# A new written-out order and a new split between VectorE and GpSimd in a polysketch attention and feed-forward kernel

## The chip, the cores and the metric

The kernel runs on one core of a Trainium2 chip. The metric is the device time of one execution in microseconds (us), the median of several runs; lower is better.

## The reference

An attention block with a polynomial sketch feeds a multiplicative feed-forward block. There are 4 batches, 4 heads, 1088 positions per batch, a head dimension of 32 and a sketch of r = 8.

```python
def phi(x):                                   # S1, S2: 8 x 32
    a = np.einsum('rd,bhsd->bhsr', S1, x)
    b = np.einsum('rd,bhsd->bhsr', S2, x)
    return np.einsum('bhsi,bhsj->bhsij', a, b).reshape(*x.shape[:-1], r * r)
q_p, k_p = phi(q), phi(k)
kv = np.einsum('bhsf,bhsd->bhfd', k_p, v)
z = np.sum(k_p, axis=2)
num = np.einsum('bhsf,bhfd->bhsd', q_p, kv)
den = np.einsum('bhsf,bhf->bhs', q_p, z)[..., None] + 1e-06
attn = num / den
...
x = attn.transpose(0, 2, 1, 3).reshape(4352, 128)
a = x @ w1                                    # 128 x 1024
b = x @ w2
out = (a * b @ w3) @ w_out                    # 1024 x 1024, 1024 x 128
```

## The kernel before

The program is a set of named steps, and each step issues a few instructions. A long table, `ORDER`, names all 1181 steps one after the other; the driver issues them so and chains the instructions of each engine in that order, so no engine ever takes a later step first. Tables beside it say on which engine a step runs and in which buffer its result lies:

```python
    def on(name):
        return pool if name in POOL else act if name in ACTS else dve

    def cp(name):
        return dve.tensor_copy if name in CPV else act.copy
...
    for name in ORDER.split():
        n = len(traced)
        steps.pop(name)()
...
            if ins.engine in last:
                tc.add_manual_dep(ins, last[ins.engine].name, behind, reason="order")
```

`dve` is VectorE, `act` ScalarE, `pool` GpSimd, `pe` TensorE. `POOL` lists the steps that GpSimd does; what is in neither `POOL` nor `ACTS` is VectorE's. `CPV` lists the copies out of PSUM that VectorE does, the others are ScalarE's. `SLOTS` holds one string for each kind of buffer: the n-th tile of that kind lies in the buffer that the n-th character names, so a tile waits until the tile that had that buffer before has been read for the last time. Kind "b" are the eight PSUM banks; "raw" are the three buffers into which weights are loaded. `WARM` gives the number of idle bf16 products (128x256) in each of the steps `warm0`, `warm1` and so on, which keep TensorE at work.

How the work is tiled:

- **k side of a batch** (`k1.` is the second batch's): load, a largest value and a leading part on a coarse grid (`k1.lead0`, L214) and the rest (`k1.rest0`, L651), Gram products (`k1.gram0` to `gram4`, L659), a chain of very small steps (G, T, N: L201, L204, L865, L898 to L937), the result `Nr` (L954), transposed keys (L720), sketches `ab` (L727) with their transposes `abt` (L745), outer products `kp` (L677), and the sums over positions `kv` (L769).
- **q side of a chunk** (`q1.` is the second half of the first batch; `q2.` and `q3.` the second batch's halves; `q4.` and `q6.` the third and fourth batch, 1024 positions wide; `qr.` what is left of all): transposed queries `tr` (L1333); `rm` (L1352); sketch products A and C with their transposes `At` (L1385) and `Ct` (L1130, L1391); then on 128-row tiles `sm`, `st`, `sh` (L1137 or L1401, L201, L204), `sl` (L1157, L1417), `sc` or `scy` and `sca` (L1165, L1161, L1421), `al` (L1170, L1426), the parts of the denominator `p01` (L1176, L1432), `p2` (L1180, L1436), `p12` (L1184, L1440), their sum `dn` (L1189, L1445), `de` and `rc` (its reciprocal), `bs` (L1204, L1459), and the outer product `phi` (L1208, L1509). For q4 and q6 a norm stands between (`na` to `nn`: L217, L1474 to L1490). `phi` is transposed by VectorE (`pT`, L1517) or TensorE (`pt`, L1246), and multiplied by kv (`x`, L1297, L1527).
- **weights**: steps `w0` to `w10`: they come as 64-bit words in pieces (`load`, on SyncE's queue, L430 to L440), and are turned into f32 by ScalarE (`c`, `m`: L263, L462, L484), VectorE (`j`: L466, L495) and GpSimd (`a`: L470, L501). Steps `w0` and `w1` make one half each of the reference's w1 and w2 together, `w2` makes w_out, `w3` to `w10` the rows of w3. `f0` to `f7` multiply w3 by w_out first (`f6.t`, L528, transposes on VectorE; `f6.m`, L534, on TensorE), so that 1024 x 128 weights are left.
- **feed-forward**: groups of 512 tokens, `g0` to `g3`, each in eight pieces of the inner dimension: `g0.4a` (L1799, x by w1), `g0.4b` (L1809, x by w2), `g0.4c` (L1804, a copy of the first out of PSUM), `g0.4m` (L1815, VectorE, their product), `g0.4o` (L1835, the second layer, summed in PSUM). `g4` to `g7` belong to the second two batches and go through a scheme with seven products in place of eight (`h4.` and `h6.`, L1673 to L1785: products, `T` and `m` sums on VectorE or GpSimd, `P` products). `gr` is the rest (L1824).

In time the kernel does the first batch's keys and queries, then g0 and g1 with the second batch, then g2, g3 and the w3 products with the third and fourth batch's keys and queries, then h4, h6 and the rest.

Of the kernel before, what the change touches and what calls it, by code (L numbers as in the profile page):

```python
# [53 lines left out]
    g4.oS g5.oS g6.oS g7.oS h4.0T2 h4.0T3 h4.0T4 h4.0m11 h4.0m12 h4.0m22 h4.1T1 h4.1T3 h4.1m11  # L54
    h4.1m12 h4.2m11 h4.2m12 h4.2m22 h4.3T4 h4.s2 h6.0T1 h6.0T2 h6.0T4 h6.0m12 h6.0m22 h6.1T1 h6.1T2
    h6.1m11 h6.1m12 h6.1m22 h6.2T4 h6.2m11 h6.2m12 h6.s1 h6.s2 h6.s4 k0.Nf k0.Nh k0.Nr k0.kp1 k1.Nr
    k1.kp1 k2.Nr k2.kp0 k2.kp1 k2.rest0 k3.Nr k3.kp0 k3.kp1 q0.al q0.p01 q0.phi1 q0.sca q1.al q1.p01
    q1.p12 q1.phi q1.sca q2.bs q2.phi0 q3.al q3.bs q3.p01 q3.p12 q3.p2 q3.phi0 q3.sc q3.sl q4.nn
# [31 lines left out]
w0.m0 g0.0a g0.3a g0.2c k1.Ta k1.Tb s.RC k2.kT1 w0.a0 q1.pt0 k1.N0 q2.tr k1.Tc k1.N1 g0.6c q2.max k1.Na g0.0c w6.load  # L90
w2.load g0.6b g0.1a q1.pt1 k2.lead0 k2.rest0 q1.pc0 q1.pc1 q2.l2 q2.l1 q3.l1 g0.1b q1.x g0.5m q1.xT g0.3c g0.1c g0.1m
w9.m k1.Nr k2.gram0 k2.gram1 k2.gram2 k2.gram3 k2.gram4 k1.Nb k2.kT0 q3.rm q2.A0 q2.rm k1.kp0 k2.ab k2.abt q2.C0 q2.C1
g1.1a g1.1c v1.loadr k2.Gm q2.At q2.sm k2.Gt q2.Ct g1.5a w9.c k3.zero q2.st q3.A0 k2.Ga q3.C0 q3.C1 q3.Ct q2.sh k2.Gb
k3.load g1.7a v.s g1.7b g1.2a v1.load g1.7c q2.sl q2.sc q2.p01 q2.al q2.p2 k2.Gc q3.At g0.0b k1.kp1 q3.sm q3.st k1.kv0
q3.sh k2.T0 k1.kv2 k1.kv3 k1.kv1 k2.T1 k1.kvr k1.kvc kr1.kp g1.2c k2.Ta q2.p12 q2.dn q2.de k2.Tb g0.0m q2.rc g0.6m
q3.sl q3.sc q3.p01 w9.j g1.7m q1.restT q2.bs g1.6a g1.6c w2.c v2.zero q2.phi0 g1.2b k3.loadr g1.3a g1.3c g1.0a g1.5b
g1.3b k1.kqt warm12 w6.c w6.m g0.3b k1.kq g1.5c g1.4a k3.max g1.4c w5.load g1.1b v2.loadr kh3.load k0.Nr q2.load g1.3m
g1.5m g1.2m g1.0c q2.pT0 warm13 g1.0b k2.Tc q2.x g0.3m w9.a1 w5.m q2.xT0 k3.kT0 k2.N0 k2.N1 w5.c q3.al q3.p2 q3.p12
q3.dn w6.j g1.0m q3.de w7.load w2.m g1.4b w7.m w7.c w3.load w10.load w4.load v2.load w2.j k2.Na g1.4m k2.Nb q3.rc
k3.kT1 k3.lead0 q2.restT q3.bs g0.2b g2.6a g2.3a g2.1a g2.5a g2.4a g2.2a w5.j g1.1m g0.2m q3.phi0 k2.Nr g2.2b g2.0a  # L100
g2.3c g2.2c g2.4b g2.5c w3.c g1.6b k3.rest0 w9.a0 g2.4c w2.a0 g2.1c w2.a1 q4.tr k3.gram0 w6.a0 w5.a1 f6.t g2.2m
k3.gram1 k3.gram2 k3.gram3 k3.gram4 q3.pT0 f6.m g2.6b g2.6c g2.0c k3.Gm v.t g2.1b k3.Gt k3.Ga k3.Gb w7.j g2.4m q4.max
g2.7a g2.3b g1.6m q4.l2 w3.m k3.Gc w7.a0 g2.0b f6.o g2.3m w5.a0 w6.a1 v3.zero g2.1m q3.x q4.l1 k3.T0 k3.T1 g2.6m w3.j
g2.7c q4.rm g2.5b g2.5m q3.xT0 q3.load g2.7b g3.0a v3.load w8.load v3.loadr k3.Ta w4.m g3.0c g3.0b g3.0m g3.3a g3.1b
g3.1a g3.3c k3.Tb w3.a0 g3.1c g2.0m k2.kp1 q6.tr k3.Tc g2.7m w7.a1 f4.t g3.6a q3.restT g3.6c q4.A0 w3.a1 q6.max k3.ab
k3.N0 k3.abt k2.kp0 q4.C0 q4.C1 k3.N1 f4.m k3.kp1 g3.6b f0.t f3.t f4.o k3.kp0 f0.m q4.At q6.l2 g3.6m k2.kv0 k2.kv3
g3.1m w4.c w4.j k3.kv0 k3.kv1 k3.kv3 k3.kv2 k3.kvr q4.Ct q4.sm q6.l1 qr.max k3.kvc k2.kv1 k2.kv2 k2.kvr k2.kvc f3.m
w8.c f0.o f3.o w4.a1 w4.a0 g3.7a g3.7c g3.4b g2.0o k3.Na q4.st f1.t qr.l2 q6.rm q4.sh w10.m qr.l1 q4.sl q4.sc g3.5a
g3.4a g3.3b f1.m f1.o w10.c g3.4c g3.4m qr.rm k3.Nb q4.p01 w8.m q4.al k3.Nr k3.kqt g2.4o q6.A0 q6.C0 f2.t g3.3m q4.p2
v.3 q6.C1 k3.kq q6.At w8.j w8.a1 q6.Ct g2.6o g3.0o g3.4o qr.A0 qr.C0 qr.C1 qr.Ct q6.sm w10.j q6.st q6.sh q4.p12 w8.a0  # L110
g3.5b q6.sl w10.a1 q6.sc q4.dn qr.At g3.5c q4.de f5.t q4.rc g1.0o g1.1o q4.na q4.bs q4.nb f2.m q4.nm q4.nr qr.sm q6.al
q6.p01 q6.p2 g0.0o g0.1o q6.p12 f2.o g0.2o g0.6o k2.kqt g0.3o q4.ne g3.5m q4.nn q6.dn k2.kq f5.m f5.o g3.7b g3.2b
g1.6o g0.5o g0.4o w10.a0 qr.st f7.t f7.m g3.2a q4.phi0 q4.phi1 qr.sh qr.sl qr.sc f7.o q4.pT0 g3.2c q4.pT1 g2.5o g0.7o
g0.oT g3.2m g3.3o g2.3o q4.x q4.xT2 q6.de qr.p01 q6.rc q4.xT0 q6.bs q6.nb q6.na g2.2o g2.7o qr.al q6.nm q6.nr q6.ne
q6.nn v.1 q4.xT1 q6.phi0 q6.phi1 g1.4o o.S3 q4.xT3 g1.2o q6.pT0 g3.5o g3.7m q6.pT1 g1.3o q6.x qr.p2 q6.xT2 qr.p12
qr.dn qr.de g3.1o g1.7o g3.6o g2.1o qr.rc qr.bs q6.xT3 g1.5o q6.xT0 h4.s1 h4.s3 q6.xT1 q6.ns g3.7o g3.2o qr.phi0
qr.pT0 g1.oT qr.x h4.0b5 h4.0a1 qr.xT0 h4.1a1 g2.oT g2.st h4.0b2 g3.oT h4.0a5 h4.0b1 h4.0bd h4.1b1 h4.0ac h4.s2 h4.s4
h4.1ac v.2 h4.0a6 h4.0bc h4.0bh h4.0ae o.S1 h6.s1 h4.0a2 h4.0ah h4.0b3 h4.1b2 o.S2 o.S4 h4.0ad h4.1a6 h6.s2 h4.0a7
h4.0m11 h4.0b6 h4.1a5 g3.st h4.1bc h4.1b6 h4.1ae h4.1bh v.4 h4.0ag h4.0be h4.0bf h4.1b5 h4.0a3 h4.0af h4.0b7 h4.1a7
h4.1be h4.1b7 h4.1ad h4.0a4 h4.0m12 h4.1a2 h4.0bg h4.1bd h4.1b3 h4.1a3 h4.0m22 h4.0b4 h4.1ag h4.2b1 h4.0ai h4.2a1  # L120
h4.1bf h4.2bc h4.2b2 h4.1ah h4.1a4 h4.2a2 h4.2ac h4.1bg h4.1af h4.1m12 h4.1m22 h4.1b4 h4.3b1 h4.2a6 h4.1ai h4.0m21
g1.st h4.2b5 h4.2ae h4.3a1 h4.2bh h4.1m11 h4.2ah h4.1m21 h4.3bc h4.1T1 h4.2m11 h4.3ac h4.2b6 h4.2be h4.2bd h4.0T1
h4.2a5 h4.2ad h4.3a2 h4.3b2 h4.3bh h4.3b6 h4.2a7 h4.2b7 h4.0T3 h4.3a6 h4.3ae h4.2ag h4.2b3 h4.3ah h4.3be h4.2a3 h4.3a5
h4.3ad h4.3b5 h4.3bd h4.2bg h4.2a4 h4.3b7 h4.3a7 h4.1T3 h4.2af h6.1b1 h4.2bf h4.3m11 h4.3a3 h4.2m22 h4.3bg h4.2b4
h4.2ai h4.3ag h4.2m12 h4.3b3 h6.0a1 h4.2m21 h6.0ac h4.3af h4.3a4 h4.1T2 h6.1bc h4.3b4 h6.1a1 h6.0b1 h6.0a6 h4.3ai
h4.3m21 h6.1b6 h4.3bf h4.2T1 h6.1ac h4.0P7 h4.2P1 h4.1P7 h4.0T2 h4.0P1 h4.0T4 h4.1P2 h4.3T1 h4.3m22 h4.1P5 h4.0P4
h6.0bc h4.2P2 h4.0P2 h4.3P5 h4.3m12 h4.2P5 h4.1P6 h4.2T2 h4.2P6 h4.0P5 h4.2T3 h4.1P1 h4.3T3 h4.3P7 h4.2P7 h4.3P1
h4.3T2 h4.3T4 h4.3P6 h4.2T4 h4.2P4 h6.0ae h4.0P6 h4.3P4 h4.1T4 h6.s3 h4.1P4 h4.k1 h4.k3 h4.3P2 h4.k2 h4.0P3 h4.3P3
h4.2P3 h4.k4 h4.k7 h4.1P3 h6.1be h4.k5 gr.1a h6.0b6 gr.1c h6.0be h6.0a7 h6.0b5 h6.0a5 h6.1a6 h6.0ad h6.1b7 h4.k8 h6.s4
# [1805 lines left out]
```

## Time and profile before

| what | value |
|---|---|
| time, median of 3 runs | 250.13 us (249.65 to 250.77) |
| the profiled execution | 248.89 us, span 246.9 us |
| TensorE (PE) busy | 238.4 us (97%) |
| VectorE (DVE) busy | 212.2 us (86%) |
| ScalarE (ACT) busy | 121.8 us (49%) |
| GpSimd (POOL) busy | 154.4 us (63%) |
| TensorE clock | 1.000 of full |
| from HBM, to HBM | 19.40 MB, 2.23 MB |

The span is from the first to the last instruction; the execution's time holds some 2 us more around it. A timeline row gives start, length, engine, line, operation, what is written and read, their shapes and the number of instructions in a run of like ones; in square brackets stands how long the engine had been idle before, and which instruction ended that. An f32 product of 128 columns by 512 appears as two records.

### The profile page before, as it was taken

The numbers are of one execution on the slowest core, as the hardware profiler recorded it, in microseconds if no ns is written. First come the engines' busy times: TensorE is split into PE (matmuls) and PEld (weight loads), VectorE is DVE, ScalarE is ACT, GpSimd is POOL, SyncE is SP. The second block draws the span as 40 slices with busy tenths as digits, with TensorE's granted clock in tenths as the row PEclk, the third lists the DMA queues.
The fourth block names the chain that finished last, engine by engine and source line by source line (L and its number), as shares of the span: only waits on it lengthen the run. The fifth ranks groups of instructions, "written<-read, shape, count | busy, mean of one in ns | idle before, by whom it ended". The sixth has DMA issues, their size and how long they took to land.

```text
span 246.9 us, 6753 instructions
## 1 busy us (share of the span) xinstructions
PE 238.4 (97%) x2726; PEld 133.7 (54%) x2726; DVE 212.2 (86%) x426; ACT 121.8 (49%) x246; POOL 154.4 (63%) x198
## 2 busy tenths in 40 slices
...
GB/s 202 267 167 324 173 204 185 92 229 135 244 177 230 183 230 142 3 4 0 3 0 0 3 1 3 54 73 4 0 0 0 3 11 74 1 0 3 0 53 96
DMA packets 31934, 22.06 MB, mean 89 GB/s; under 512 B 21280, under 2 KB 26528, under 8 KB 31904
## 3 DMA queue, kind: packets, MB, share of 16 engines
...
q8 instruction: 21, 0.34, 0.6%
...
HBM read 19.40 MB, written 2.23 MB: 88 GB/s over the span
## 4 chain that ended last, share of the span: by engine, by line
PE 80%; DVE 15%; issue 2%; POOL 1%; ACT 0%; DVEq 0%
PE ps_X L1673 11%; PE ps_o L1759 10%; PE a_ps L1799 9%; PE b_ps L1809 9%; PE ps_o L1835 9%; PE ps_w3o L534 6%; PE ps_Y L1673 6%; PE idle_ps L255 4%; PE ps_Z L1673 3%; DVE ab L1815 3%; PE ps_g L659 2%; PE ps_ac L1374 2%; PE ps_kv L769 2%; PE ps_or L1824 2%; DVE pT L1517 1%
## 5 line engine op out<-in xcount | busy, mean ns | idle before, releaser
L1809 PE MATMUL b_ps<-xT,w 128*128 128x512 f32 (+1 forms) x80 | 36.4, 560 | 0.3 <-DVE ab L1815 0.2
L1673 PE MATMUL ps_X<-xd,wv 64*128 64x512 f32 x112 | 35.6, 595 | 0.0
L1799 PE MATMUL a_ps<-xT,w 128*128 128x512 f32 (+1 forms) x80 | 35.4, 558 | 0.0
L1804 ACT COPY ffa<-a_ps 128x512 f32<-128x512 f32 (+1 forms) x34 | 17.6, 536 | 30.4 <-PE a_ps L1799 30.3
L1680 ACT COPY hc<-ps_X 128x512 f32<-128x512 f32 x37 | 20.7, 589 | 21.2 <-PE ps_X L1673 12.9
L1835 PE MATMUL ps_o<-ab,w3o 128*128 128x512 f32 x64 | 29.4, 597 | 0.0
L1815 DVE TENSOR_TENSOR ab<-ffa,b_ps 128x512 f32<-128x512 f32 (+1 forms) x40 | 23.9, 619 | 3.2 <-PE b_ps L1809 2.5
L501 POOL TENSOR_TENSOR w3c<-w3c,cv_m 128x512 int32<-128x512 int32 x16 | 21.0, 1328 | 6.3 <-DVE w3c L495 6.3
L1799 PEld LDWEIGHTS a_ps<-xT,w 128*128 128x128 f32 x80 | 14.4, 190 | 14.6 <-issue 8.5
L1707 POOL TENSOR_TENSOR hc<-hc 128x512 f32<-128x512 f32 x15 | 19.7, 1327 | 2.9 <-DVE hc L1685 2.9
L1673 PEld LDWEIGHTS ps_X<-xd,wv 64*128 64x128 f32 x112 | 15.2, 186 | 10.4 <-issue 8.3
L1809 PEld LDWEIGHTS b_ps<-xT,w 128*128 128x128 f32 x80 | 14.0, 190 | 12.2 <-issue 7.7
L1673 PE MATMUL ps_Y<-xd,wv 64*128 64x512 f32 x48 | 19.2, 599 | 0.0
L1835 PEld LDWEIGHTS ps_o<-ab,w3o 128*128 128x128 f32 x64 | 11.7, 190 | 13.7 <-issue 13.2
L534 PEld LDWEIGHTS ps_w3o<-wo,w3T 128*128 128x128 f32 x128 | 15.3, 192 | 3.2 <-issue 2.5
L534 PE MATMUL ps_w3o<-wo,w3T 128*128 128x128 f32 x128 | 15.9, 277 | 0.6 <-DVE w3T L528 0.6
L1540 ACT COPY xd<-ps_x 64x256 f32<-64x256 f32 x32 | 11.7, 367 | 7.6 <-PE ps_x L1527 7.2
L538 ACT COPY w3o<-ps_w3o 128x128 f32<-128x128 f32 x8 | 2.0, 270 | 26.3 <-PE ps_w3o L534 26.3
L1759 PE MATMUL ps_o<-hc,w3o 128*64 128x512 f32 x32 | 14.7, 596 | 0.0
L1848 POOL TENSOR_TENSOR oT<-oT,nz 128x512 f32<-128x512 f32 x4 | 4.2, 1049 | 15.6 <-DVE oT L1842 14.4
L263 ACT ACTIVATE cv_c<-raw 128x1024 f32<-128x1024 f32 (+1 forms) x13 | 13.0, 1010 | 1.5 <-DMA raw<-in_moe_w_dram 1.5
L1509 POOL TENSOR_TENSOR ph<-s_al,s_bs 128x1024 f32<-128x1024 f32 x5 | 10.4, 2096 | 4.6 <-issue 4.5
...
## 6 DMA issues: line engine op xcount, KB each, us to landing
...
```

The lines of the kernel that those rows point to most:

```text
L263: act.activation(dst, hi.bitcast(F32), ACT.Prelu, scale=2.0 ** -112, alpha=-2.0 ** 32)
L501: pool.tensor_tensor(d, d, x["m"][:, i * 512:(i + 1) * 512], ALU.add)
L534: pe.matmul(t["o"], w3T[ko][:, c], wo[:, c], start=c == 0, stop=c == NC - 1)
L1673: pe.matmul(x[bank], stat(j, u)[:, i * 128:(i + 1) * 128], rows(j, u), start=new, stop=True, tile_position=(u * 64, 0), skip_group_check=True)
L1680: cp(n(y))(x[k], x[bank])
L1707: on(f"h{g}.{i}m{k}").tensor_mul(both[0][k], both[0][k], both[1][k])
L1759: pe.matmul(acc_o[bank][half[0]:half[1]], w(i), x(i), start=n == 1, stop=n == (2 if j == 3 else 4), tile_position=(0, half[0]), skip_group ...
L1799: pe.matmul(x["a"][:, :w], w_of(0, c), xT[g][:, c0:c0 + w], start=True, stop=True)
L1804: cp(f"g{g}.{c}{su}c")(x["s"][:, :w], x["a"][:, :w])
L1809: pe.matmul(x["b"][:, :w], w_of(1, c), xT[g][:, c0:c0 + w], start=True, stop=True)
L1815: dve.tensor_mul(ab_sb[g, c][:, c0:c0 + w], x["s"][:, :w], x["b"][:, :w])
L1835: pe.matmul(o_ps[g], w3o[:, c], ab_sb[g, c], start=n == 1, stop=n == NC)
```

## The change

Only tables change. `ORDER` is the same up to the step `q0.xT1`, that is until the first chunk of queries, q0, is through; behind it all steps stand in a new order. The first instructions that differ run at about 26.7 us. `POOL`, `CPV` and `SLOTS` go with the new order: 29 steps move from VectorE to GpSimd, 18 from GpSimd to VectorE, 12 copies from ScalarE to VectorE and 10 from VectorE to ScalarE. The planner that wrote the tables counted with long holds between VectorE and GpSimd. The last two entries of `WARM`, one idle product each, are gone with their steps.

```diff
-WARM = [27, 2, 3, 4, 4, 4, 1, 2, 1, 1, 2, 2, 1, 1]
+WARM = [27, 2, 3, 4, 4, 4, 1, 2, 1, 1, 2, 2]
...
-    "raw": "012012021020121",
+    "raw": "012011012121202",
...
 POOL = set("""
...
-    q4.p2 q4.phi0 q4.phi1 q4.sc q6.al q6.p12 q6.phi1 q6.sc q6.sl qr.p01 qr.p12 s.KS s.Pp s.blk
+    q3.p12 q3.p2 q3.phi0 q3.sc q4.al q4.p01 q4.p12 q4.p2 q4.phi0 q4.phi1 q4.sl q6.bs q6.p12 q6.p2
...
-w0.load k1.lead0 q0.xc0 q0.xc1 k0.kq w1.a1 k2.max q0.xt1 k1.ab q0.xT0 q0.xT1 g0.4a q1.load g0.5a q1.sm q1.Ct q1.st
-q1.sh k1.rest0 w0.m1 g0.4b g0.6a q1.sl q1.scy q1.sca g0.7a q1.p01 q1.al k1.abt k1.gram0 k1.gram1 k1.gram2 k1.gram3
+w0.load k1.lead0 q0.xc0 q0.xc1 k0.kq w1.a1 k2.max q0.xt1 k1.ab q0.xT0 q0.xT1 g0.4a q1.load s.RC g0.5a q1.sm q1.st
+k1.abt g0.4b k1.rest0 q1.sh g0.7a q1.Ct w0.c1 g0.4c w0.c0 kr1.abc w0.m1 k1.gram0 g0.7c k1.gram1 q3.tr k1.gram2 w0.j1
...
```

Three places show what moves. The first is VectorE from 26.3 us on, at the second half of the first batch's queries (s_g, s_t, s_hl, s_pr), the second batch's keys (kk, kabt) and a weight (w_81, j). Before:

```order
L1137 TENSOR_REDUCE s_g<-ps_a 128x32
L1130 STREAM_TRANSPOSE ay_C<-ps_c 128x384
L201 SCALAR_TENSOR_TENSOR s_t_699<-s_g,ps_a 128x256
L204 SCALAR_TENSOR_TENSOR s_hl<-s_g,s_t_699 128x2x128
L651 TENSOR_TENSOR kk<-k,kk 128x1152
L1157 TENSOR_TENSOR s_hl<-ps_a,s_hl 128x2x128
L1165 TENSOR_TENSOR s_hl<-s_hl,ay_C 128x128
L745 STREAM_TRANSPOSE kabt<-ps_ab 128x256 x2
L1180 TENSOR_TENSOR s_pr<-s_al,s_hl 128x128
L466 TENSOR_SCALAR w_81<-cv_c 128x2x256
L1333 STREAM_TRANSPOSE qT<-qh 128x512
L217 TENSOR_REDUCE G_g<-ps_g 128x1
```

In the changed kernel:

```order
L1137 TENSOR_REDUCE s_g<-ps_a 128x32
L201 SCALAR_TENSOR_TENSOR s_t_700<-s_g,ps_a 128x256
L745 STREAM_TRANSPOSE kabt<-ps_ab 128x256 x2
L651 TENSOR_TENSOR kk<-k,kk 128x1152
L204 SCALAR_TENSOR_TENSOR s_hl<-s_g,s_t_700 128x2x128
L1130 STREAM_TRANSPOSE ay_C<-ps_c 128x384
L1333 STREAM_TRANSPOSE qT<-qh 128x512
L466 TENSOR_SCALAR w_81<-cv_c 128x2x256
L1157 TENSOR_TENSOR s_hl<-ps_a,s_hl 128x2x128
L1165 TENSOR_TENSOR s_hl<-s_hl,ay_C 128x128
L1176 TENSOR_TENSOR s_pr<-s_hl 128x256
L466 TENSOR_SCALAR w_81<-cv_c 128x2x256
```

The transposes kabt and ay_C, kk and qT and the weight step change places with q1's chain: s_hl (L1157) was the sixth step and is now the ninth, and the product s_pr (L1176) is new here.

The second place is GpSimd at the same time, where q1's chain (s_hl, s_pr, s_al, ph) meets weights (w_81, a) and the second and third batches' kk (L651). Before:

```order
L470 TENSOR_TENSOR w_81<-w_81,cv_m 128x2x256 x2
L1161 TENSOR_TENSOR s_hl<-s_hl,ay_C 128x128
L1176 TENSOR_TENSOR s_pr<-s_hl 128x256
L1170 TENSOR_TENSOR s_al<-s_hl 128x128
L1184 TENSOR_TENSOR s_pr<-s_pr 128x128
L470 TENSOR_TENSOR w_81<-w_81,cv_m 128x2x256
L577 MEMSET v 64x4x32
L1208 TENSOR_TENSOR ph<-s_al,s_bs 128x1024
L378 COPY RC<-Sc 128x4x8 x3
L470 TENSOR_TENSOR w_81<-w_81,cv_m 128x2x256
L651 TENSOR_TENSOR kk<-k,kk 128x1152
```

In the changed kernel:

```order
L470 TENSOR_TENSOR w_81<-w_81,cv_m 128x2x256 x2
L378 COPY RC<-Sc 128x4x8 x3
L1161 TENSOR_TENSOR s_hl<-s_hl,ay_C 128x128
L1170 TENSOR_TENSOR s_al<-s_hl 128x128
L1180 TENSOR_TENSOR s_pr<-s_al,s_hl 128x128
L1184 TENSOR_TENSOR s_pr<-s_pr 128x128
L470 TENSOR_TENSOR w_81<-w_81,cv_m 128x2x256
L1204 TENSOR_TENSOR s_bs<-ay_C,s_rc 128x128
L1208 TENSOR_TENSOR ph<-s_al,s_bs 128x1024
L954 TENSOR_TENSOR AR<-RC,mask2n 128x2x8
L577 MEMSET v 64x4x32
L470 TENSOR_TENSOR w_81<-w_81,cv_m 128x2x256
```

The copies RC come first, s_pr (L1176) has gone, and s_pr (L1180) and s_bs (L1204) have come from VectorE, the latter just ahead of ph.

The third place is VectorE at the fourth batch's queries, q6: the norm (s_d, nz), the outer product ph and its transposes pT. Before, behind the transposes of q4:

```order
L1459 TENSOR_TENSOR s_bs<-ay_C,s_rc 128x256
L217 TENSOR_REDUCE s_d<-s_bs 128x32
L217 TENSOR_REDUCE s_d<-s_al 128x32
L1426 TENSOR_TENSOR s_al<-s_hl 128x64
L1474 TENSOR_TENSOR s_d<-s_d 128x32
L1480 TENSOR_REDUCE nz<-s_d 128x8
L1484 TENSOR_SCALAR nz<-nz 128x8
L1485 TENSOR_SCALAR nz<-nz 128x8
L1490 TENSOR_TENSOR s_bs<-s_bs,nz 128x256
L1509 TENSOR_TENSOR ph<-s_al,s_bs 128x1024
L1517 STREAM_TRANSPOSE pT<-ph 128x1024
L1815 TENSOR_TENSOR ab<-ffa,b_ps 128x512
```

In the changed kernel, from the second transpose of q4 on:

```order
L1517 STREAM_TRANSPOSE pT<-ph 128x1024
L217 TENSOR_REDUCE s_d<-s_bs 128x32
L1474 TENSOR_TENSOR s_d<-s_d 128x32
L1480 TENSOR_REDUCE nz<-s_d 128x8
L1484 TENSOR_SCALAR nz<-nz 128x8
L1485 TENSOR_SCALAR nz<-nz 128x8
L1490 TENSOR_TENSOR s_bs<-s_bs,nz 128x256
L1509 TENSOR_TENSOR ph<-s_al,s_bs 128x1024
L1517 STREAM_TRANSPOSE pT<-ph 128x1024
L1445 TENSOR_REDUCE s_d<-s_pr 128x2x8
L1517 STREAM_TRANSPOSE pT<-ph 128x1024
```

The steps s_bs (L1459) and s_al (L1426) are gone from VectorE here, a sum (L217) lies further ahead, and g3.7m (L1815) stood between the two last transposes and now stands behind them.

More of the change, by code (lines that the diff above doesn't have):

```diff
@@ L53 @@
 POOL = set("""
[L54 to L58, printed above, removed]
-    q4.p2 q4.phi0 q4.phi1 q4.sc q6.al q6.p12 q6.phi1 q6.sc q6.sl qr.p01 qr.p12 s.KS s.Pp s.blk
-    s.blkh s.low s.rest
+    g4.oS g6.oS g7.oS h4.0T1 h4.0T2 h4.0T3 h4.0m11 h4.0m12 h4.0m22 h4.1T3 h4.1m11 h4.1m12 h4.1m22
+    h4.2T3 h4.2m12 h4.2m22 h4.s2 h4.s3 h4.s4 h6.0T1 h6.0T2 h6.0T3 h6.0m12 h6.0m22 h6.1T1 h6.1T3
+    h6.1m11 h6.1m12 h6.1m22 h6.2T3 h6.2T4 h6.2m11 h6.2m22 h6.s2 h6.s3 h6.s4 k0.Nf k0.Nh k0.Nr k0.kp1
+    k1.Nr k1.kp0 k1.kp1 k2.kp0 k2.kp1 k2.rest0 k3.Nr k3.kp0 k3.kp1 q0.al q0.p01 q0.phi1 q0.sca q1.al
+    q1.bs q1.p12 q1.p2 q1.phi q1.sca q1.sl q2.al q2.p01 q2.p2 q2.phi0 q2.sc q2.sl q3.al q3.bs q3.p01
+    q3.p12 q3.p2 q3.phi0 q3.sc q4.al q4.p01 q4.p12 q4.p2 q4.phi0 q4.phi1 q4.sl q6.bs q6.p12 q6.p2
+    q6.phi1 qr.al qr.bs qr.p01 qr.p12 qr.p2 qr.phi0 qr.sc s.KS s.Pp s.blk s.blkh s.low s.rest
 """.split())
@@ L90 @@
[L90 to L129, printed above, removed]
@@ new lines @@
+q1.sl k1.gram3 q1.scy k1.gram4 k1.Gc q1.sca q1.p01 g0.6b kh2.load w0.j0 g0.4m g0.6a q3.max q1.al q1.p2 q1.p12 q1.dn
+k1.Gm g0.5c w0.a1 g0.2a g0.0a k1.Gt q1.de q1.rc s.AR w0.m0 k1.Ga k1.Gb k1.T0 q1.bs q1.phi k1.T1 k2.lead0 g0.3a g0.0c
+k0.Nr g0.5b w2.load q3.l2 v2.zero g0.7b k2.kT1 w9.load g0.2c q1.pt0 w6.load k1.Ta k1.Tb g0.6c g0.3c k1.Tc k1.N0 w2.m
+k1.N1 w0.a0 g0.1a k2.kT0 q1.restT k1.Na q2.tr g0.1c k2.rest0 q1.pt1 g0.1b q1.pc0 q1.pc1 q1.x k2.gram0 k2.gram1 q2.max
+k1.kp1 k1.Nb q2.l2 g0.1m g0.5m k3.zero k3.load g0.7m k1.Nr k2.gram2 k2.gram3 q3.l1 q2.l1 q3.rm k2.gram4 q1.xT w6.c
```

91 lines of the change are left out of this document (63 added, 28 removed).

## The prediction

> **What bounds the kernel now.** I read the page first: busy times, then the chain that ended last.
>
> ```profile
> PE 238.4 (97%) x2726; PEld 133.7 (54%) x2726; DVE 212.2 (86%) x426; ACT 121.8 (49%) x246; POOL 154.4 (63%) x198
> PE 80%; DVE 15%; issue 2%; POOL 1%; ACT 0%; DVEq 0%
> ```
>
> TensorE is at work for 238.4 of 246.9 us, at full granted clock, and 80% of the chain is its own. The change leaves every product in place except two idle ones. So the time can only move by TensorE's waits, and by how often VectorE (86%) or GpSimd (63%) comes late. The windows say in which stages that is:
>
> ```profile
> 140.00:151.00 11.00, 9.52 (x143) 4.12 (x142) 9.74 (x22) 5.87 (x17) 4.74 (x8) 1.00 0.01 2
> 151.00:247.00 96.00, 92.20 (x478) 46.14 (x478) 80.59 (x132) 36.94 (x79) 60.56 (x72) 1.00 0.14 24
> 240.74 2.50 PE L1824 MATMUL ps_or<-w3o,ab 128*128 128x128 f32 x20
> ```
>
> Columns of the first two: window, length, then busy time of PE, PEld, DVE, ACT, POOL. The third row is TensorE's last one in its timeline. Between 140 and 151 us TensorE stands for 1.5 us. From 151 us on it lacks 3.8, and 3.7 of that lie behind its last product, which ends at 243.24 of 246.9: in the stage itself it practically never waits. The timeline of TensorE gives the single waits, and a row without one gives the rhythm:
>
> ```profile
> 69.60 4.03 PE L1799 MATMUL a_ps<-xT,w 128*128 128x512 f32 x9
> 38.62 0.24 PE L912 MATMUL ps_N<-T_p,P2a 32*32 32x8 f32 x8 [0.22 <-DVE T_p L204]
> 44.10 0.34 PE L659 MATMUL ps_g<-kk 128*32 128x64 f32 x8 [0.60 <-POOL kk L651]
> 73.86 1.12 PE L1809 MATMUL b_ps<-xT,w 128*128 128x512 f32 x2 [0.23 <-DVE ab L1815]
> 79.99 2.02 PE L534 MATMUL ps_w3o<-wo,w3T 128*128 128x128 f32 x16 [0.60 <-DVE w3T L528]
> 148.41 0.76 PE L1527 MATMUL ps_x<-pT,kq 32*32 32x256 f32 x16 [1.09 <-DVE ab L1815]
> 149.56 1.36 PE L1527 MATMUL ps_x<-pT,kq 32*32 32x256 f32 x48 [0.39 <-DVE pT L1517]
> ```
>
> Nine records in 4.03 us each some 0.59 long (1.02 for two, in a row further below, less 0.43): they start (4.03 − 0.59) / 8 = 0.43 us apart and a product, two records, costs 0.86. A record's end is drawn 0.16 after the next could start, so a wait is 0.16 to 0.17 longer than its bracket: 0.39, 0.76, 0.40, 0.77, 1.26 and 0.55. That is 4.1 us, all that a better order can win here. The last two, 1.81 us at q6.x, are the largest.
>
> Behind several of them stands not work but a hold: VectorE and GpSimd stop each other.
>
> ```profile
> 37.06 0.18 DVE L201 SCALAR_TENSOR_TENSOR T_t<-T_g,ps_T 32x32 f32<-32x32 f32 x1
> 37.26 1.26 POOL L470 TENSOR_TENSOR w<-w,cv_m 128x512 int32<-128x512 int32 x1
> 37.27 1.29 DVE L204 SCALAR_TENSOR_TENSOR T_p<-T_g,T_t 32x32 f32<-32x32 f32 x1
> 131.38 3.96 POOL L1509 TENSOR_TENSOR ph<-s_al,s_bs 128x1024 f32<-128x1024 f32 x2
> 133.57 1.93 DVE L1417 TENSOR_TENSOR s_hl<-ay_A,s_hl 128x128 f32<-128x128 f32 x1
> 135.53 0.29 DVE L1421 TENSOR_TENSOR s_hl<-s_hl,ay_C 128x128 f32<-128x128 f32 x1
> ```
>
> T_t reads PSUM and takes 0.18; T_p, as small but with both inputs in SBUF, starts with GpSimd's w0.a0 and ends with it: 1.29, a hold of 1.1. s_hl at 133.57 ends as GpSimd's second phi does, and its like takes 0.29 right behind: a hold of 1.64. The Trainium skill ("SBUF — State Buffer", section "Who interferes with whom") calls the port pair of the two an exclusive lock; by that rule each of these rows is one lock held to the end, and the trace agrees.
>
> **The change part by part.** *The early part, q1 and the second batch's keys (26.7 to 45 us).* VectorE's durations for the steps it now does, in other order:
>
> ```profile
> 26.66 0.57 DVE L1130 STREAM_TRANSPOSE ay_C<-ps_c 128x384 f32<-128x384 f32 x1
> 27.16 0.38 DVE L201 SCALAR_TENSOR_TENSOR s_t<-s_g,ps_a 128x256 f32<-128x256 f32 x1
> 27.58 0.42 DVE L204 SCALAR_TENSOR_TENSOR s_hl<-s_g,s_t 128x256 f32<-128x256 f32 x1
> 27.92 1.35 DVE L651 TENSOR_TENSOR kk<-k,kk 128x1152 f32<-128x1152 f32 x1
> 29.19 0.42 DVE L1157 TENSOR_TENSOR s_hl<-ps_a,s_hl 128x256 f32<-128x256 f32 x1
> 29.64 0.29 DVE L1165 TENSOR_TENSOR s_hl<-s_hl,ay_C 128x128 f32<-128x128 f32 x1
> 29.85 0.77 DVE L745 STREAM_TRANSPOSE kabt<-ps_ab 128x256 f32<-128x256 f32 x2
> 31.72 0.42 DVE L466 TENSOR_SCALAR w<-cv_c 128x512 int32<-128x512 int32 x1
> 32.05 0.70 DVE L1333 STREAM_TRANSPOSE qT<-qh 128x512 f32<-128x512 f32 x1
> 34.95 1.28 DVE L1815 TENSOR_TENSOR ab<-ffa,b_ps 128x512 f32<-128x512 f32 x2
> 28.35 1.02 PE L1809 MATMUL b_ps<-xT,w 128*128 128x512 f32 x2
> 31.02 0.34 PE L659 MATMUL ps_g<-kk 128*32 128x64 f32 x8
> 32.84 1.98 PE L1809 MATMUL b_ps<-xT,w 128*128 128x512 f32 x4
> ```
>
> From 26.66: s_t 0.38, kabt 0.77, kk 1.35, s_hl 0.42, ay_C 0.57, qT 0.70, w 0.42, then q1.sl (L1157) 0.42 ends at 31.7, where before it ended at 29.6. Behind it: 0.29, p01 (L1176, new on VectorE, both inputs in SBUF, taken as 0.42), w 0.42, g0.4m 0.64: 33.5, and 34.1 with one hold by q1.sca on GpSimd (0.56, its row below). TensorE meanwhile does g0.4b (to 29.2), g0.7a, the Gram products (32.84 − 31.02 = 1.82), g0.6b: 32.8. Its next product g0.6a takes the PSUM bank that g0.4m reads, and so waits 1.3. Before, g0.6a stood ahead of the Gram products and waited for nothing.
>
> ```profile
> 29.68 0.56 POOL L1161 TENSOR_TENSOR s_hl<-s_hl,ay_C 128x128 f32<-128x128 f32 x1 [2.09 <-DVE s_hl L1157]
> 34.84 2.01 POOL L1208 TENSOR_TENSOR ph<-s_al,s_bs 128x1024 f32<-128x1024 f32 x1 [1.03 <-DVE s_bs L1204]
> 40.45 0.88 DVE L214 TENSOR_SCALAR kk<-k,k_g 128x1152 f32<-128x1152 f32 x1
> 41.40 2.65 POOL L651 TENSOR_TENSOR kk<-k,kk 128x1152 f32<-128x1152 f32 x1 [2.88 <-DVE kk L214]
> 35.76 0.69 ACT L462 ACTIVATE cv_m<-raw 128x512 int32<-128x512 uint32 x1
> ```
>
> GpSimd then: q1's chain, w0.a1 (1.26) and q1.bs end near 36.7. VectorE's k2.lead0 (0.88, to 37.6) gets in ahead of q1.phi (2.01, to 39.6 or 39.7), k1.Nr and w0.a0 (1.26) end near 41.6, k2.rest0 (2.65) near 44.4. On TensorE g0.5b waits for VectorE's copy g0.0c, behind k2.lead0 (0.88 + 0.64 behind 36.7, near 38.4): 0.4; g0.1a waits for w0.a0: 0.6; then transposes, g0.1b and q1.x end near 44.9, and k2.gram0 starts there, after k2.rest0. Before it started at 44.10: **+0.8** in all, the old 0.39 and 0.76 taken off already.
>
> *Middle, 45 to 120 us.* Both rows at 73.86 and 79.99 wait for VectorE. In the new order it stands about 2 us further on there, since q2's sl, sc, al, p01 and p2 now lie on GpSimd: −0.40 − 0.77 = **−1.17**. My walk through the rest, step by step with before's durations, leaves three places where the releaser comes behind TensorE: q2.x and g2.5b 0.15 each, f4.m 0.3: **+0.6**. That is an estimate from differences of long sums, and so anywhere from 0 to twice that. The loads: SP now sends kh2, w2, w9, w6 in place of w9, kh2, w6, w2. w6 takes the buffer that w0.m0 (ACT, 35.76 before) reads out, so it starts near 36.5 and must be there for ACT near 45.5. I set it at nothing; if it came late, ACT, with 51% of its time free, would hold a few copies by about 1 us.
>
> *Third and fourth batch's queries, q4 and q6, 120 to 151 us.* Now q6's chain up to its norm comes before q4's transposes, q6.bs moves from VectorE to GpSimd, and q6.x lies two products earlier on TensorE (five of the ps_o products went behind it, three ahead). TensorE arrives near 147.15 − 2 × 0.86 = 145.4. GpSimd does q4.phi0, q4.phi1 and q6.phi1 (1.98 each from the row at 131.38) with q6.bs, two wv steps of 1.26 as w0.a0 and five small ones between: 11 us from 130.4 to 141.4. Then pT1, qr.de, qr.rc and g3.7m on VectorE end near 143.9, which leaves 1.5 us. q4.x is six products earlier, near 135.3; my sum for q4.pT1 is 134.3. So both waits of q6.x go: **−1.81**. What is next late: nothing for 1.0 to 1.5 us.
>
> *From 151 us on.* The planner moved many T, m and s steps between VectorE and GpSimd; VectorE has 15.4 us free in that window (96 − 80.59) and arrives 2 to 3.5 us earlier by my sums, but TensorE did not wait there before: 0, by ± 0.3. The two idle products that are taken out are 256 columns wide; by the 0.43 of a 512-column record one is worth at most 0.2, so 0 to −0.4 together. I take nothing: they stand ahead of g0.3b and g1.0b, where a small wait of the walk may open in their place, and the granted clock is 1.00 with them.
>
> **Sum:** +0.8 − 1.17 + 0.6 − 1.81 = −1.6 us. The profiled execution took 248.89, so 247.3; it lies 1.24 below the median of 250.13, and on that scale the forecast is **248.5**.
>
> **Rivals.**
> *More is won.* g0.4m is not held and g0.6a waits 0.1 instead of 1.3, and all that follows it moves up: −2.8 at most, 247.3. For it: the hold needs q1.sca to start within the same half us. Against: VectorE's other late steps are independent of that.
> *Same time.* VectorE is held twice ahead of q4.x as in the rows above, 1.1 + 1.64 = 2.7, more than the 1.0 it has: +1.7, net +0.1, 250.2. For it: GpSimd's share of work grew there (q6.p2, bs, qr.sc, al); against: those are fewer VectorE steps with both inputs in SBUF.
> *Slower.* GpSimd goes first at each handover and becomes the bound. If q1.phi starts before k2.lead0, that step waits its 2.01 less what has passed, and k2.rest0 with the Gram products is about 1.2 later; ahead of q6.x its 11 us chain stretches by two holds of the size VectorE shows (1.64 each, 3.3, less the 1.5 of spare: +1.8). Net −1.6 + 1.2 + 1.8 = +1.4, 251.5. It decides at the moment when k2.lead0 is ready: before q1.phi or not. For it: GpSimd took 29 steps from VectorE and gave 18, and its row at 41.40 idles 2.88 before that step, a cover that is gone; against: VectorE was free for long stretches after its own work moved.
> The Trainium skill ("Perfetto Trace Analysis", section "Optimizing Scalar/DVE Operations") warns that work moved between those two might not help, as they share a port; by it this third case would be the likely one, and the holds above agree that the port is shared.
>
> **How the numbers follow.** A measurement here tells about 0.5%, 1.25 us, from no change. The forecast gets 0.34 and the larger gain 0.08: faster 0.42. The case of equal time gets 0.27, the slower 0.31. The forecast's own range is 247.6 to 249.4 (0.6 for the small waits, 0.3 for the end). The whole reaches from the larger gain less 0.4 to the slower case plus 0.8 for a late load or a third hold: 246.9 to 252.3.
>
> **What would show it.** Right: a wait of over 1 us at the product g0.6a near 33 us, k2.gram0 near 44.9, no wait at q4.x and q6.x, k2.lead0 ahead of q1.phi. Wrong: GpSimd's phi before k2.lead0, a wait at q6.x from q6.pT1 or g3.7m, a new wait behind a load, or VectorE rows of over 1 us for 0.3 us steps before q4.x; and any wait over 0.5 us behind 151 us, where I set nothing.

## The result and the profile after

The changed kernel is faster: 247.16 us median against 249.65 of before on the same chip, a ratio of 0.990 (95% interval 0.987 to 0.993). Three of the changed kernel's nine runs were longer at a lower granted clock (0.985 to 0.993); the ratio leaves them out, the median does not. The profiled execution took 246.63 us with a span of 244.8; before it was 248.89 and 246.9. The page and the two windows that were shown of before now read:

```profile
PE 236.8 (97%) x2724; PEld 133.1 (54%) x2724; DVE 210.7 (86%) x420; ACT 121.0 (49%) x241; POOL 163.6 (67%) x209
PE 83%; DVE 10%; DMA 2%; POOL 1%; ACT 1%; issue 1%; POOLq 0%; DVEq 0%
...
140.00:151.00 11.00, 11.00 (x87) 4.89 (x86) 6.12 (x12) 6.61 (x19) 9.06 (x8) 1.00 0.01 2
151.00:245.00 94.00, 90.28 (x475) 45.94 (x474) 81.19 (x130) 32.17 (x66) 61.25 (x75) 1.00 0.14 24
```

GpSimd is busy 9 us longer, VectorE 1.5 less, and TensorE has no idle time left between 140 and 151 us. TensorE's timeline shows where it waits now: q4.x and q6.x, the last two rows, start without a wait (a bracket would stand behind the row), and four new waits stand in the early part.

```profile
33.35 1.12 PE L1799 MATMUL a_ps<-xT,w 128*128 128x512 f32 x2 [0.56 <-DVE ab L1815]
34.81 1.98 PE L1799 MATMUL a_ps<-xT,w 128*128 128x512 f32 x4 [0.34 <-POOL w L470]
46.37 0.25 PE L1365 MATMUL ps_ac<-q,AR 64*32 64x128 bf16 x8 [0.45 <-ACT xT L1302]
48.77 0.51 PE L1374 MATMUL ps_ac<-q,RC 32*32 32x128 f32 x32 [1.20 <-DVE q L1352]
136.08 1.50 PE L1527 MATMUL ps_x<-pT,kq 32*32 32x256 f32 x64
146.28 1.50 PE L1527 MATMUL ps_x<-pT,kq 32*32 32x256 f32 x64
```

With the 0.16 that a record overhangs, the four are 0.72 (g0.6a), 0.50 (g0.2a), 0.62 (q2.A0) and 1.36 (q2.C1). The waits of before at 38.62, 44.10, 73.86, 79.99, 148.41 and 149.56 are gone.

Where the time went is read most safely from the start of the same product in both timelines ("lag" is its start after the change less its start before), at places ahead of which both orders have done the same products (but for the two idle ones):

| product | before | after | lag |
|---|---|---|---|
| g0.4a, the first behind the common part | 26.56 | 26.24 | −0.32 |
| k2.gram0 | 44.10 | 44.03 | −0.07 |
| q3.A0 | 49.45 | 51.13 | +1.68 |
| q2.x | 65.18 | 66.31 | +1.13 |
| q3.x | 86.23 | 86.43 | +0.20 |
| f0.m | 99.82 | 100.33 | +0.51 |
| qr.x | 157.06 | 155.63 | −1.43 |
| end of the last product | 243.24 | 241.28 | −1.96 |

The first line is no part of the change: the code up to there is the same, and it begins with waits for loads and differs by up to 1.5 us among the runs below. So the change costs 2.0 us up to 51 us, wins 0.55 up to 66 and 0.9 up to 86, loses 0.3, wins 1.9 at q4 and q6 and 0.5 behind 157 us.

### The profile page after: what moved, and what is told of

The parts are those of the page before. It is cut to its first block, busy times and chain, and to the rows that moved or that the text cites. A ratio compares the mean times of both kernels' runs of the same rounds, so it can differ in the third digit from the quotient of the medians.

```text
span 244.8 us, 6771 instructions
## 1 busy us (share of the span) xinstructions
PE 236.8 (97%) x2724; PEld 133.1 (54%) x2724; DVE 210.7 (86%) x420; ACT 121.0 (49%) x241; POOL 163.6 (67%) x209
## 4 chain that ended last, share of the span: by engine, by line
PE 83%; DVE 10%; DMA 2%; POOL 1%; ACT 1%; issue 1%; POOLq 0%; DVEq 0%
PE a_ps L1799 12%; PE ps_o L1835 11%; PE ps_X L1673 11%; PE ps_o L1759 10%; PE b_ps L1809 9%; PE ps_Y L1673 6%; PE ps_w3o L534 5%; PE ps_Z L1673 3%; DVE ab L1815 2%; PE ps_ac L1374 2%; DMA k<-in_k_dram 2%; PE ps_x L1527 2%; PE ps_kv L769 2%; PE ps_or L1824 2%; PE idle_ps L255 1%; DVE q L1352 1%
## 5 line engine op out<-in xcount | busy, mean ns | idle before, releaser
L1799 PE MATMUL a_ps<-xT,w 128*128 128x512 f32 (+1 forms) x80 | 36.3, 564 | 1.0 <-DVE ab L1815 0.6
L1673 PE MATMUL ps_X<-xd,wv 64*128 64x512 f32 x112 | 37.1, 592 | 0.0
L1804 ACT COPY ffa<-a_ps 128x512 f32<-128x512 f32 (+1 forms) x32 | 16.8, 546 | 34.6 <-PE a_ps L1799 28.2
L1680 ACT COPY hc<-ps_X 128x512 f32<-128x512 f32 x33 | 18.5, 590 | 18.5 <-PE ps_X L1673 13.8
L1815 DVE TENSOR_TENSOR ab<-ffa,b_ps 128x512 f32<-128x512 f32 (+1 forms) x40 | 23.3, 618 | 2.2 <-PE b_ps L1809 2.2
L1707 POOL TENSOR_TENSOR hc<-hc 128x512 f32<-128x512 f32 x15 | 18.9, 1275 | 4.1 <-DVE hc L1685 4.1
L1673 PE MATMUL ps_Y<-xd,wv 64*128 64x512 f32 x48 | 20.7, 591 | 0.0
L1509 POOL TENSOR_TENSOR ph<-s_al,s_bs 128x1024 f32<-128x1024 f32 (+1 forms) x6 | 12.9, 2149 | 3.9 <-DVE s_bs L1459 2.6
L1540 ACT COPY xd<-ps_x 64x256 f32<-64x256 f32 x28 | 10.3, 367 | 7.4 <-PE ps_x L1527 7.0
L1759 PE MATMUL ps_o<-tt,ws 128*64 128x512 f32 x32 | 13.3, 600 | 0.0
L1759 PE MATMUL ps_o<-hc,ws 128*64 128x512 f32 x32 | 11.8, 595 | 0.0
```

Of the source, the lines that this page charges most:

```text
L1673: pe.matmul(x[bank], stat(j, u)[:, i * 128:(i + 1) * 128], rows(j, u), start=new, stop=True, tile_position=(u * 64, 0), skip_group_check=True)
L1680: cp(n(y))(x[k], x[bank])
L1707: on(f"h{g}.{i}m{k}").tensor_mul(both[0][k], both[0][k], both[1][k])
L1759: pe.matmul(acc_o[bank][half[0]:half[1]], w(i), x(i), start=n == 1, stop=n == (2 if j == 3 else 4), tile_position=(0, half[0]), skip_group ...
L1799: pe.matmul(x["a"][:, :w], w_of(0, c), xT[g][:, c0:c0 + w], start=True, stop=True)
L1804: cp(f"g{g}.{c}{su}c")(x["s"][:, :w], x["a"][:, :w])
```

## Experiments

All ratios are to before on the same chip, with 95% intervals. "Lag" is as in the table above, with the common part's own difference taken off. In three kernels (the one without idle products, the first with the old early part, the first mended one) the line numbers are 9 or 10 lower, as their tables take fewer lines.

**The two idle products, alone.**

```diff
-WARM = [27, 2, 3, 4, 4, 4, 1, 2, 1, 1, 2, 2, 1, 1]
+WARM = [27, 2, 3, 4, 4, 4, 1, 2, 1, 1, 2, 2]
```

> The kernel before, without the two idle products warm12 and warm13 and nothing else changed. Theory (the terms of the trace add up): in the trace of before the next product starts 0.33 us behind warm12 and 0.11 behind warm13, so 0.44 us go: ratio 0.998. Rival (they stand where TensorE would have waited anyway): 0, ratio 1.000, and the 0.33 shows as a wait of the product behind k1.kqt.

Ratio 0.999 (0.997 to 1.001), which holds both the theory's 0.998 and the rival's 1.000; the trace decides, and it is neither as the theory nor as the rival had it. Some 0.47 us were there from 65 us on, and were gone behind one product:

```profile
73.41 1.12 PE L1799 MATMUL b_ps<-xT,w 128*128 128x512 f32 x2 [0.71 <-DVE ab L1805]
```

This is g2.2b, whose wait for VectorE was 0.23 in the bracket and is now 0.71. In before's plan VectorE is the bound there, so whatever TensorE wins ahead of it comes back as a wait.

**The idle products put back into the changed kernel.** `warm12` behind `k1.kqt` and `warm13` behind `g1.1b`.

> The changed kernel with the two idle products put back behind k1.kqt and g1.1b. In before, taking them out won nothing: the 0.44 us came back as a longer wait at 73.4 us. Theory (a term counts where no wait comes behind it): the changed kernel has no wait of TensorE on VectorE near there, so the two products cost it their 0.2 to 0.4 us: 0.2 to 0.4 above the changed kernel in the trace at 70 us and still at the end. Rival (given back again): the offset is there at 70 us and gone by 105 us, behind the small waits at 89 and 103 us.

The theory held: the lag to the changed kernel, the 0.45 of the common part not taken off, grew by 0.44 behind the two (from 0.46 to 0.90), was 1.0 at 75 us and 1.14 at the end. That is a cost of 0.44 at their place and 0.7 at the end. The ratio to before rose to 0.995 (0.993 to 0.998). So the same edit is worth nothing in one plan and 0.4 to 0.7 us in the other.

**One wait on GpSimd in the changed kernel.** In the changed kernel's timelines of VectorE and GpSimd:

```profile
45.67 3.05 DVE L1352 SCALAR_TENSOR_TENSOR q<-q,qT 128x512 f32<-128x512 bf16 x2
46.21 1.96 POOL L677 TENSOR_TENSOR kp<-kabt 128x1024 f32<-128x1024 f32 x1
```

Two steps on VectorE, 0.65 each elsewhere, end half a microsecond behind GpSimd's k1.kp0, and TensorE's q2.C1 waits for the second.

In the driver, `made` holding each step's instructions:

```diff
+HELD = [('k1.kp0', 'q2.rm')]
...
+    for late, early in HELD:
+        tc.add_manual_dep(made[late][0], made[early][-1].name, landed, reason="held back")
```

> The changed kernel with one more wait: GpSimd's k1.kp0 may start only when VectorE's q2.rm is done. Theory (hold): in the changed kernel the two steps of L1352 took 3.05 us instead of about 1.3, because k1.kp0 ran from 46.21 to 48.17; without the overlap the wait of 1.36 us at q2.C1 (48.77) goes, and the kernel is 1.4 us faster than the changed one, about 3.5 below before in the profile (ratio about 0.984). Rival (VectorE and GpSimd bound the middle): the wait goes, but k1.kp0 and what follows it on GpSimd comes 1 to 2 us later and TensorE gets the time back as new waits before 115 us: no change against the changed kernel, ratio 0.99.

Ratio 0.985 (0.982 to 0.989), near the theory's 0.984. The steps and the product, in the same timelines:

```profile
45.43 1.29 DVE L1352 SCALAR_TENSOR_TENSOR q<-q,qT 128x512 f32<-128x512 bf16 x2
...
46.80 1.95 POOL L677 TENSOR_TENSOR kp<-kabt 128x1024 f32<-128x1024 f32 x1 [0.78 <-DVE q L1352]
...
47.08 0.75 PE L1374 MATMUL ps_ac<-q,RC 32*32 32x128 f32 x32
```

1.29 in place of 3.05, and no wait at q2.C1. The lag to the changed kernel fell by 1.47 there, and 1.03 was left at the end, since 0.2 each came back near 50 and at k3.kv. So the hold itself is shown, and its price is mostly real, with a third given back.

**The same kind of wait in the kernel before, at q6.** `HELD = [('q6.phi1', 'q6.phi0')]`. Before, the two ran side by side; in the changed kernel too, but there VectorE's started first:

```profile
143.40 1.95 POOL L1509 TENSOR_TENSOR ph<-s_al,s_bs 128x1024 f32<-128x1024 f32 x1 [4.47 <-issue]
143.57 2.86 DVE L1509 TENSOR_TENSOR ph<-s_al,s_bs 128x1024 f32<-128x1024 f32 x1 [0.30 <-DVE s_bs L1490]
```

```profile
138.66 1.23 DVE L1509 TENSOR_TENSOR ph<-s_al,s_bs 128x1024 f32<-128x1024 f32 x1
138.71 3.00 POOL L1509 TENSOR_TENSOR ph<-s_al,s_bs 128x1024 f32<-128x1024 f32 x1 [0.36 <-DVE s_bs L1490]
```

> The kernel before with one more wait: GpSimd's q6.phi1 may start only when VectorE's q6.phi0 is done. Theory (hold): in before the two ran at the same time, and VectorE's took 2.86 us instead of 1.2 to 1.4; alone it ends near 144.9, pT0 near 146.1, g3.7m near 148.0 or earlier, and of the 1.81 us that TensorE stands at q6.x about 1.2 go: ratio 0.995. Rival (GpSimd's part decides): q6.phi1 ends 1.4 us later, near 146.8, q6.pT1 cannot start before that, and q6.x gets in the second wait what it saves in the first: ratio 1.000, the sum of both waits still 1.6 or more.

Ratio 0.9954 (0.9940 to 0.9969), as the theory had it, and 1.34 us less lag behind q6.x. In VectorE's and TensorE's timelines:

```profile
143.68 1.23 DVE L1509 TENSOR_TENSOR ph<-s_al,s_bs 128x1024 f32<-128x1024 f32 x1 [0.30 <-DVE s_bs L1490]
147.03 1.25 DVE L1517 STREAM_TRANSPOSE pT<-ph 128x1024 f32<-128x1024 f32 x1 [0.20 <-POOL ph L1509]
...
147.35 0.66 PE L1527 MATMUL ps_x<-pT,kq 32*32 32x256 f32 x16
148.33 1.36 PE L1527 MATMUL ps_x<-pT,kq 32*32 32x256 f32 x48 [0.32 <-DVE pT L1517]
```

The first wait at q6.x is gone, the second is 0.48 in place of 0.55. One added wait, which stops nothing but GpSimd, gives half of what the whole new plan gives.

**The new split alone, and the new order alone.** The first has the `POOL` and `CPV` tables of the changed kernel in before's order; the second has before's tables in the new order.

> The kernel before with the new POOL and CPV tables alone: its own order and buffers, the changed kernel's engines for every step. Theory (order and split belong together; the gain comes from what stands where): steps moved to GpSimd stand behind other GpSimd work that the old order put there, TensorE waits at more places: slower than before by 1 to 5 us, ratio 1.004 to 1.02. Rival (the new split of the work is the gain, since VectorE gets 2.6 us less to do): faster by 1 us or more, ratio 0.996 or less.

> The changed kernel with the old POOL and CPV tables: the new order and buffers, the old engines. Theory (order and split belong together): slower than the changed kernel by 1 to 5 us, ratio to before 0.995 to 1.01. Rival (the new order is the gain, the split indifferent): as the changed kernel, 0.99.

Ratios 1.111 (1.107 to 1.114) and 1.071 (1.069 to 1.074). Both theories had the sign and were far too small. In the first the largest single wait was 4.65 us at qr.x; GpSimd's and VectorE's rows there:

```profile
166.12 3.54 POOL L1497 COPY nz<-nz 32x8 f32<-32x8 f32 x16
169.74 1.07 POOL L1509 TENSOR_TENSOR ph<-s_al,s_bs 128x512 f32<-128x512 f32 x1
...
170.84 0.71 DVE L1517 STREAM_TRANSPOSE pT<-ph 128x512 f32<-128x512 f32 x1 [6.29 <-POOL ph L1509]
171.70 1.61 PE L1527 MATMUL ps_x<-pT,kq 32*32 32x64 f32 x56 [4.49 <-DVE pT L1517]
```

qr.phi0, now GpSimd's, stands behind sixteen small copies that the old order had put ahead of it when it was VectorE's. Losses like this are spread over the whole span (5 us by 61, 10 by 136, 18 by 167, 27 at the end). Order and split are one plan, and neither half of it alone is worth anything.

**Five steps of q2 back on VectorE in the changed kernel.** `sl`, `sc`, `al`, `p01` and `p2` of q2 taken out of `POOL`.

> The changed kernel with five steps of q2 (sl, sc, al, p01, p2) on VectorE again. Theory (the prediction's reason for the middle): VectorE does 5 steps or about 2 us more near 52 to 57 us, and the waits at 74 and 80 us that the change took away come back: slower than the changed kernel by 1 us or more. Rival (VectorE is ahead for other reasons, above all the order): less than 0.3 us.

Ratio 0.999 (0.996 to 1.002): the steps are worth what the theory said (1.1 us by 62, 1.6 at the end), but not where it said. The waits at 74 and 80 us did not come back; TensorE came to those products 1.1 us later than in the changed kernel, so the run does not tell whether they would have without that. Instead TensorE waited earlier, for a PSUM bank that VectorE's copy of k1.kvc reads out:

```profile
60.62 1.13 PE L1799 MATMUL a_ps<-xT,w 128*128 128x512 f32 x2 [0.72 <-DVE kvc L799]
```

The last 0.5 came at k3.kv, near 105.6 us, behind a wait of 0.53 whose cause stays open.

**The old early part with the new later part.** Before's order and engines up to g1.7a, and in a second version up to k2.gram0 to gram4; behind that the changed kernel's, without idle products.

> Order, engines and copies as in the kernel before up to g1.7a (50.6 us), behind it the changed kernel's order and engines for all steps that are left; without the two idle products. Theory (terms add): the early part of the change cost 2.0 us, the rest won 3.6 (0.5 in the middle, 2.2 at q4 and q6, 0.44 idle products, 0.5 behind 151 us): before less 3.6, ratio 0.985, 1.5 below the changed kernel. Rival (the later gain needs the early part's head start on VectorE and GpSimd): the wait at q6.x or those at 74 and 80 us come back, ratio 0.99 or more.

> As the first kernel with the old early part, but with the seam at k2.gram4 and buffers chosen so that only 33 tiles lie elsewhere than in the two parents (357 of the 454 tiles behind the seam did in the first). Theory (the first one was slow by its buffers): within 1% of the changed kernel, ratio 0.98 to 1.00. Rival (the old early part does not fit the new later part): still over 1.03.

Ratios 1.058 (1.054 to 1.062) and 1.0045 (1.002 to 1.0075). The second fits no theory exactly. That buffers are a third leg of the plan, beside order and split, is likely but not shown: seam and buffers both differ between the two, so how much of the first one's loss is the buffers' alone is open. In the second the old early part is 1.8 us ahead of the changed kernel when q3.A0 starts, near the 2.0 of the lag table, and 1.2 ahead once that step has waited 0.5 for VectorE in its midst; it is 2.6 us behind at the end. Half of the 3.8 that it loses from there on is one wait at k2.kv0, of 2.1 (the changed kernel has 0.24 at k3.kv0 close by), whose releaser the profile does not name. GpSimd's outer products (kp), which these products read, had ended at 102.01, so it was not they:

```profile
105.55 0.66 PE L769 MATMUL ps_kv<-kp,v 128*32 128x64 f32 x33 [1.96 <-issue]
```

So part of the early 2.0 us bought something later; which step it was stays open.

**The changed kernel with its early waits mended.** The first version:

```diff
 VectorE:  g0.4m ahead of q1.p01 and w0.j0; w0.j1 ahead of q3.tr; q2.rm ahead of q3.rm
 ScalarE:  w0.m1 right behind w0.c1; q2.l1, then q1.xT, then q3.l1
 GpSimd:   w0.a1 ahead of q1.sca
+HELD = [('k1.kp0', 'q3.rm')]
```

The second adds `w0.m0` right behind `w0.c0` (ScalarE) and `w0.a0` ahead of `q1.bs` (GpSimd).

> The changed kernel with its four early waits mended: g0.4m ahead of q1.p01 and w0.j0 on VectorE; w0.j1 ahead of q3.tr, w0.m1 right behind w0.c1, w0.a1 ahead of q1.sca; q1.xT's copy ahead of q3.l1 on ScalarE, q2.rm ahead of q3.rm, and k1.kp0 not before q3.rm. Theory (terms add): waits of 0.72, 0.50, 0.62 and 1.36 us go, 0.2 comes at k2.gram0, so 2.9 below the changed kernel, about 5.0 below before in the profile: ratio 0.98. Rival (given back later): TensorE is early, VectorE and GpSimd are not, and waits of 1 to 3 us come up between 55 and 115 us: ratio 0.985 to 0.99.

> The changed kernel with its early waits mended further: all edits of the first mended version, and w0.m0 right behind w0.c0 on ScalarE, w0.a0 ahead of q1.bs on GpSimd, so that the rest step of the next keys (k2.rest0) comes earlier and no longer stands on VectorE's small step L204, which took 2.30 us instead of 0.16 there. Theory (terms add): the waits of 0.39 at g0.1a and 0.88 at q2.A0 go, 1.2 us below the first mended version, about 4.9 below before in the profile: ratio 0.981. Rival (VectorE and GpSimd bound the middle by now): new waits between 55 and 150 us take back half or more: ratio 0.984 or above.

Ratios 0.9858 (0.982 to 0.989) and 0.9827 (0.980 to 0.985): the second is the fastest here, 244.81 us median, and below the changed kernel's interval. The first lies in its rival's range, the second between its theory (0.981) and its rival (0.984). Against the changed kernel the second's lag fell by 2.2 us, not the 3.2 of the four waits. Two waits are left, 0.38 at g0.0a and 0.42 at k3.kv; the rest of the difference came back in smaller pieces. By its trace the first version won 1.8 and the single added wait 1.0, but by their times these two cannot be told apart (0.9858 and 0.9853); the second version lies below both, with intervals that overlap theirs. The mended step in the first version and in the second, VectorE's row and GpSimd's:

```profile
39.70 2.30 DVE L195 SCALAR_TENSOR_TENSOR RC<-N_g,N_t 128x8 f32<-128x8 f32 x1
...
39.36 2.62 POOL L642 TENSOR_TENSOR kk<-k,kk 128x1152 f32<-128x1152 f32 x1
```

```profile
40.93 0.92 DVE L204 SCALAR_TENSOR_TENSOR RC<-N_g,N_t 128x8 f32<-128x8 f32 x1
...
39.17 2.65 POOL L651 TENSOR_TENSOR kk<-k,kk 128x1152 f32<-128x1152 f32 x1
```

It still stands behind k2.rest0 until 41.8, but for 0.92 us in place of 2.30.

## Why the prediction was right, point by point

The forecast was −1.6 us, and the whole range held the result. By the medians beside each other it is −2.5; 247.16 lies below the forecast's own range (247.6 to 249.4), next to the 247.3 of the larger gain. The profile gives −2.1, of which 0.3 lie ahead of the change. Of the five terms only that of q4 and q6 has the measured size. The others missed by −0.55 (early part), +1.15 (middle and idle products together) and −0.5 (the end), and the common part gave another −0.3. That these nearly cancel is luck.

- **q4 and q6, −1.81 forecast: right in size and direction, and half named.** Between f0.m and qr.x the lag fell by 1.94, and both waits at q6.x are gone. As forecast, VectorE's chain for q6 runs earlier: q6.phi0 starts at 138.66 in place of 143.57, while q6.x comes only 2.1 us earlier. What the forecast did not name is that before, q6.phi0 itself was held by GpSimd (2.86 in place of 1.23); the added wait in before, which takes that hold away, wins 1.34 alone.
- **The early part to k2.gram0, +0.8 forecast, +0.25 measured (the common part's −0.32 taken off).** The wait at g0.6a was 0.72 and not 1.3, those at g0.5b and g0.1a did not come, and one of 0.50 came at g0.2a instead.
- **The middle from k2.gram0 on, −1.17 + 0.6 forecast, +0.58 measured up to f0.m with the idle products' −0.44 in it: the step that failed.** It failed in its first 6 us: from k2.gram0 to q3.A0 the change costs 1.75, where the walk put no wait at all. There k1.kp0, new on GpSimd, held q2.rm (1.36), and q1.xT's copy behind q3.l1 and q2.l1 held a PSUM bank (0.62). I had looked for holds where steps had changed places on VectorE, and this step was in its old place; what had moved was its neighbour on the other engine. With the early part's 0.25 that is the 2.0 of the table; the second mended version wins back 2.2.
- **The middle behind q2.x: right in size, wrong in reason.** From q2.x to f0.m the lag fell by 0.62, with both waits gone and small ones of 0.25 and less in their place. The forecast had VectorE 2 us further on there. Its rows, first before and then in the changed kernel, show the order at work instead (before, g2.2b waits for g1.1m and f6.m for f6.t; L1815 is g1.1m, L528 is f6.t, and L495 is the weight step w5.j):

```profile
70.93 2.29 DVE L495 TENSOR_SCALAR w3c<-cv_c 128x1024 int32<-128x1024 int32 x1
73.14 1.27 DVE L1815 TENSOR_TENSOR ab<-ffa,b_ps 128x512 f32<-128x512 f32 x2
78.65 1.19 DVE L528 STREAM_TRANSPOSE w3T<-w3c 128x1024 f32<-128x1024 f32 x1
```

```profile
68.10 0.68 DVE L1815 TENSOR_TENSOR ab<-ffa,b_ps 128x512 f32<-128x512 f32 x1
80.05 0.69 DVE L495 TENSOR_SCALAR w3c<-cv_c 128x1024 int32<-128x1024 int32 x1
81.38 1.23 DVE L528 STREAM_TRANSPOSE w3T<-w3c 128x1024 f32<-128x1024 f32 x1
```

  g1.1m comes 5 us earlier, ahead of w5.j and not behind it, and g2.2b stands five products later on TensorE. f6.t comes 2.7 us later, not earlier; three more products stand ahead of f6.m, which now starts about 0.1 us late at most. How much of VectorE's room for this is owed to q2's five steps is not shown.
- **The idle products, 0 forecast, −0.44 measured by putting them back.** "A wait may open in their place" is what happens in before, and not in the changed kernel.
- **Behind 151 us, 0 ± 0.3 forecast, −0.5 measured,** in steps of 0.1 to 0.35 between 170 and 225 us.
- **The larger gain** needed g0.6a to wait 0.1; it waited 0.72. The result came near that rival's number for other reasons.
- **The rival of equal time** needed two holds of together 2.7 us ahead of q4.x. In VectorE's rows there the tiny steps L1474 and L1484 take 0.71 and 0.52 in place of 0.19 and 0.17, and q4.x does not wait.
- **The slower rival** was decided in VectorE's and GpSimd's rows at the place it named:

```profile
35.40 0.87 DVE L214 TENSOR_SCALAR kk<-k,k_g 128x1152 f32<-128x1152 f32 x1
35.65 2.44 POOL L1208 TENSOR_TENSOR ph<-s_al,s_bs 128x1024 f32<-128x1024 f32 x1
```

k2.lead0 came first, and it was q1.phi that took 2.44 in place of 2.01. Ahead of q6.x GpSimd's phi did lose 1.05 us (3.00 in place of 1.95), less than the spare. The split alone made the kernel slower (ratio 1.111), with its largest wait owed to GpSimd's queue and not to a hold; with an order made for it the kernel gained although GpSimd's busy time rose by 9 us. The Trainium skill ("Perfetto Trace Analysis", section "Optimizing Scalar/DVE Operations") warns that work moved between the two might not help, as they share a port; here it depended on the order.
